# Global-local attention and a gated two-matmul block: the two matmuls in separate phases, attention beside the second

## The chip, the cores and the metric

The kernel runs on one core of a Trainium2 chip. The metric is the device time of one execution in microseconds (us). Times are medians of four or more executions; in the same rounds the kernel before is run on the same chip. The profile is of one execution; its span is about 1.7 us shorter than the time. Engines are named as the profile names them: PE is TensorE's matmuls, PEld its weight loads, DVE is VectorE, ACT is ScalarE, POOL is GpSimd, SP the queue that issues the value loads and the output stores. PSUM is the memory that matmuls write to. The granted clock is the share of full speed that the profile records for TensorE's clock.

## The reference, cut to what matters

```python
# attention: 8 batches, 8 heads, 512 local tokens, 32 global tokens, head size 64
k_all = concat([k_g, k_l]); v_all = concat([v_g, v_l])
out_g = softmax(scale * q_g @ k_all.T) @ v_all              # global rows see everything
s_ll  = where(|i - j| <= 32, scale * q_l @ k_l.T, -1e9)     # local rows: a band, and the global keys
out_l = softmax(concat([scale * q_l @ k_g.T, s_ll])) @ v_all
x = concat([out_g, out_l])                                  # 8*544 tokens x 512
# the block
h = x @ w_in                                                # 512 -> 2048
g = h * sigmoid(1.702 * h)
out = g @ w_out                                             # 2048 -> 512
```

The kernel treats the 512 local tokens of a batch as one block of 512 columns, eight blocks in all, and gathers the global tokens of all batches (256 columns) in a ninth.

## The kernel before

Each batch is two "quads" of four heads, `a` and `c`. A quad's attention is a chain over four engines: transposes `T` of keys and queries (DVE), scores `S` in two rounds (PE), exponentials `X` (ACT), band mask `M` (DVE), then value products `U(0)` (the softmax sums), `U(1)`, `U(2)` (the two halves of the values) and `Gm` (global rows), all on PE, each read out of PSUM by DVE or ACT: `R1`/`R2` turn `U(0)` into reciprocals, `XL` scales `U(1)` and `U(2)` into `x`, `G1` to `G3` do it for `Gm`.

The block has 16 `h` steps (four matmuls into one PSUM bank, a tanh on ACT, a multiply on DVE) and 16 `o` steps (four matmuls each; four steps accumulate in one bank, which ACT then copies to `ob` for the store).

The kernel uses eight PSUM banks, divided so:

```python
psS = tile_pool("psS", bufs=4, PSUM)   # scores
psV = tile_pool("psV", bufs=1, PSUM)   # value products U(0), U(1), U(2), Gm: one bank
psH = tile_pool("psH", bufs=2, PSUM)   # h
psO = tile_pool("psO", bufs=1, PSUM)   # o
```

Everything is interleaved, step by step. In step `k` one `h` step, one `o` step that lies 24 steps behind it, and a piece of attention of the batch after follow each other:

```python
def step(k, pe=(), act0=(), act1=(), dve=()):
    h_mm(k)
    for f in pe: f()              # attention on PE
    if k >= LAG: o_mm(k - LAG)    # LAG = 24
    ...
    h_tanh(k)
    ...
    h_mul(k)
    ...
def att_table(b):
    ...                           # [cut: scores in steps 0 to 7]
    P(5, lambda: a.U(0));   V(5, lambda: a.R1())
    P(7, lambda: a.U(1));   V(8, lambda: a.XL(0))
    P(9, lambda: a.U(2));   V(9, lambda: a.XL(1))
    P(10, lambda: a.Gm());  V(10, lambda: a.G1())
    P(11, lambda: c.U(0));  ...
    V(14, lambda: quads(n)[0].T(0)); V(15, lambda: quads(n)[0].T(1))
```

The loads are issued in the order batch 0, `w_in`, batch 1, `w_out`, then the global keys, queries and values of all later batches in three large pieces (`load_g(4, NQ)`).

The softmax here doesn't subtract the row's maximum and nothing guards it: scores larger than these inputs give would overflow.

## Time and profile before

The median is 424.98 us (423.78 to 425.44, four runs).

| quantity | value | where it is read |
|---|---|---|
| PE busy share of the span | 79% | page, part 1 |
| share of PE in the chain that ended last | 60% | page, part 4 |
| period of a batch | 44.5 us | start of the `rs` transpose of quad `a`, batches 3 to 7, mean of four |
| PE busy in a period | about 38 us | table of windows |
| granted clock at 50 to 89 us | 0.56 | table of windows |

The period is read in every kernel in the same way: each batch transposes its reciprocals once for quad `a` (`rs<-rT` on DVE), and the distance of these marks from batch 3 to batch 7 is divided by four. In before they lie at 144.67 and 322.59 us.

The first fence is the page: the span, PE's busy time, and PE's busy tenths and granted clock in 40 slices of the span. The second is the first line of the chain that ended last.

```profile
span 422.8 us, 7348 instructions
...
PE 335.5 (79%) x2915; PEld 176.1 (42%) x2960; DVE 227.1 (54%) x396; ACT 200.4 (47%) x387; POOL 95.8 (23%) x169
...
PE   0488572578888978899689968998699789999984
...
PEclk9999955599989998999999998999999899999999
```

```profile
PE 60%; DMA 10%; POOL 8%; ACT 8%; issue 6%; DVE 6%; DVEq 0%; POOLq 0%; ACTq 0%
```

PE is the engine that decides, but a fifth of the span it is idle, and in slices 6 to 8 (53 to 85 us) the clock is at half.

Next the waits of PE in the steady part, 150 to 300 us (engine, what it wanted to do, the releaser: total, times, longest), and three of them in the timeline (start, duration, engine, line, operation; in brackets the idle time ahead of it and its releaser).

```profile
PE ov L295 <- DVE xL L323: 9.2, 8, 2.0
PE ov L295 <- ACT xg L345: 7.3, 4, 1.8
PE s L245 <- DVE qT L223: 4.9, 3, 1.6
```

```profile
157.20 0.23 PE L295 MATMUL ov<-e_1801,onesBD 128*128 128x160 bf16 x1 [1.83 <-ACT xg L345]
...
166.00 0.23 PE L295 MATMUL ov<-e_1801,vgU_156 128*128 128x160 bf16 x1 [2.01 <-DVE xL L323]
...
174.27 0.48 PE L245 MATMUL s<-qT,kT 32*128 32x160 bf16 x16 [1.62 <-DVE qT L223]
```

The value products wait for `xL` and `xg`.

The start-up has another wait. These are DVE in the timeline, the issue of the large global load (KB, then us from issue to landing), and a table of windows (start:end, length, busy us and instructions of PE, PEld, DVE, ACT, POOL, granted clock, DMA share, GB/s).

```profile
64.65 0.31 DVE L155 STREAM_TRANSPOSE kgT<-rkg 128x128 bf16<-128x128 bf16 x1 [6.44 <-DMA rkg<-in_k_g_dram]
67.19 0.31 DVE L155 STREAM_TRANSPOSE qgT<-rqg 128x128 bf16<-128x128 bf16 x1 [2.23 <-DMA rqg<-in_q_g_dram]
```

```profile
rkg<-in_k_g_dram POOLq DMA_DIRECT2D x1, 192.0 KB, 17.1
```

```profile
core 0: us, PE busy (x) PEld busy (x) DVE busy (x) ACT busy (x) POOL busy (x), PEclk, DMA share, GB/s
50.00:89.00 39.00, 21.10 (x260) 13.61 (x261) 20.65 (x37) 13.45 (x28) 20.43 (x36) 0.56 1.41 165
146.30:191.60 45.30, 39.03 (x360) 20.00 (x362) 27.02 (x44) 23.85 (x47) 9.15 (x16) 0.96 0.44 71
191.60:235.20 43.60, 37.32 (x356) 19.46 (x358) 26.99 (x44) 23.83 (x47) 9.14 (x16) 1.00 0.48 74
```

DVE stands for 6.4 us in front of the transposed global keys of batch 2, and the attention of batch 1 comes behind them in DVE's program: PE's wait for its `sT`, 7.0 us, ends at 69.29 us.

### The profile page before, as it was taken

The numbers are of one execution on the slowest core, as the hardware profiler recorded it, in microseconds if no ns is written. First come the engines' busy times: TensorE is split into PE (matmuls) and PEld (weight loads), VectorE is DVE, ScalarE is ACT, GpSimd is POOL, SyncE is SP. The second block draws the span as 40 slices with busy tenths as digits, with TensorE's granted clock in tenths as the row PEclk, the third lists the DMA queues.
The fourth block names the chain that finished last, engine by engine and source line by source line (L and its number), as shares of the span: only waits on it lengthen the run. The fifth ranks groups of instructions, "written<-read, shape, count | busy, mean of one in ns | idle before, by whom it ended". The sixth has DMA issues, their size and how long they took to land.

```text
span 422.8 us, 7348 instructions
## 1 busy us (share of the span) xinstructions
PE 335.5 (79%) x2915; PEld 176.1 (42%) x2960; DVE 227.1 (54%) x396; ACT 200.4 (47%) x387; POOL 95.8 (23%) x169
## 2 busy tenths in 40 slices
PE   0488572578888978899689968998699789999984
PEld 0363251335434534454345534454355344445531
DVE  3666835389446653775467645664565433433200
ACT  1546661278336743574456643773466225343311
POOL 8958814981016100620043000000000000000000
PEclk9999955599989998999999998999999899999999
DMA  9799999993009400880069001400001000110122
GB/s 159 82 192 145 142 180 175 157 109 33 26 2 189 61 26 25 126 126 25 26 97 155 26 26 31 119 26 25 2 26 48 3 26 33 43 48 28 50 76 50
DMA packets 83315, 31.16 MB, mean 74 GB/s; under 512 B 75856, under 2 KB 77904, under 8 KB 83280
## 3 DMA queue, kind: packets, MB, share of 16 engines
q0 software_dynamic: 44496, 13.38, 30.0%
q1 hardware_dynamic: 38784, 17.31, 17.2%
q8 instruction: 23, 0.38, 0.4%
q14 instruction: 12, 0.10, 0.1%
HBM read 35.13 MB, written 8.91 MB: 104 GB/s over the span
## 4 chain that ended last, share of the span: by engine, by line
PE 60%; DMA 10%; POOL 8%; ACT 8%; issue 6%; DVE 6%; DVEq 0%; POOLq 0%; ACTq 0%
PE op L393 26%; PE hp L367 21%; DMA rvg<-in_v_g_dram 5%; PE s L268 4%; DMA w_in_sb<-in_moe_w_in_dram 3%; ACT xg L345 3%; PE ov L302 3%; POOL rq L78 3%; POOL rk L78 3%; PE s L245 2%; PE ov L295 2%; DMA rq<-in_q_l_dram 2%; DVE xL L323 2%; DVE qT L223 2%; ACT th L375 1%
## 5 line engine op out<-in xcount | busy, mean ns | idle before, releaser
L381 DVE SCALAR_TENSOR_TENSOR gT<-th,hp 128x512 bf16<-128x512 f32 (+1 forms) x144 | 94.1, 654 | 118.0 <-ACT th L375 117.5
L375 ACT ACTIVATE th<-hp 128x512 f32<-128x512 f32 (+1 forms) x144 | 82.8, 575 | 133.4 <-PE hp L367 132.8
L393 PE MATMUL op<-w_out_sb,gT 128*128 128x512 bf16 x508 | 136.0, 386 | 7.7 <-ACT ob L403 4.7
L367 PE MATMUL hp<-xL,w_in_sb 128*128 128x512 bf16 x503 | 131.3, 387 | 2.1 <-DVE xL L323 1.1
L367 PEld LDWEIGHTS <-w_in_sb 128*128 128x128 bf16 x576 | 57.1, 100 | 67.5 <-issue 6.5
L393 PEld LDWEIGHTS <-gT 128*128 128x128 bf16 x544 | 50.2, 98 | 58.1 <-issue 9.2
L78 POOL DMA_DIRECT2D rk<-in_k_l_dram x64 | 37.0, 582 | 102.4 <-DVE kT L223 91.7
L245 PE MATMUL s<-qT,kT 32*128 32x160 bf16 (+1 forms) x496 | 19.2, 253 | 31.4 <-DVE qT L223 29.3
L78 POOL DMA_DIRECT2D rq<-in_q_l_dram x64 | 36.7, 578 | 24.1 <-DVE qT L223 9.6
L403 ACT ACTIVATE ob<-op 128x512 f32<-128x512 f32 x34 | 20.4, 601 | 31.3 <-PE op L393 31.0
L245 PEld LDWEIGHTS <-kT 32*128 32x128 bf16 x512 | 11.3, 98 | 45.6 <-issue 22.8
L345 ACT ACTIVATE xg<-og,rg 32x64 bf16<-32x64 f32 x64 | 19.4, 303 | 22.3 <-DVE rg L337 21.6
L323 DVE TENSOR_TENSOR xL<-ov,rs 128x512 bf16<-128x512 f32 x32 | 21.9, 687 | 9.4 <-PE ov L302 9.2
L223 DVE STREAM_TRANSPOSE kT<-rk 128x1024 bf16<-128x1024 bf16 x16 | 20.8, 1300 | 3.6 <-DMA rk<-in_k_l_dram 3.6
L223 DVE STREAM_TRANSPOSE qT<-rq 128x1024 bf16<-128x1024 bf16 x16 | 20.9, 1304 | 2.4 <-DMA rq<-in_q_l_dram 2.4
L311 DVE STREAM_TRANSPOSE sT<-ov 128x512 f32<-128x512 f32 x16 | 11.4, 714 | 7.5 <-PE ov L302 7.5
L295 PEld LDWEIGHTS <-onesBD 128*128 128x128 bf16 x64 | 6.0, 106 | 18.0 <-issue 15.1
L295 PEld LDWEIGHTS <-vgU_164 128*128 128x128 bf16 x48 | 4.6, 108 | 18.5 <-issue 17.2
L318 DVE STREAM_TRANSPOSE rs<-rT 128x512 f32<-128x512 f32 x16 | 11.3, 704 | 0.1
L268 PEld LDWEIGHTS <-kT 128*128 128x128 bf16 x128 | 8.1, 103 | 6.2 <-issue 4.5
L367 PE MATMUL hp<-xG,w_in_sb 128*128 128x256 bf16 x64 | 9.6, 273 | 0.1
L189 POOL DMA_DIRECT2D w_in_sb<-in_moe_w_in_dram x16 | 8.5, 536 | 4.7 <-DMA w_in_sb<-in_moe_w_in_dram 4.3
(363 smaller groups left out, 327.5 us busy)
## 6 DMA issues: line engine op xcount, KB each, us to landing
vst<-in_v_l_dram SPq DMA_DIRECT2D x64, 128.0 KB, 5.6
out_dram<-ob SPq DMA_DIRECT2D x32, 256.0 KB, 2.0
rk<-in_k_l_dram POOLq DMA_DIRECT2D x64, 64.0 KB, 4.1
rq<-in_q_l_dram POOLq DMA_DIRECT2D x64, 64.0 KB, 3.8
w_in_sb<-in_moe_w_in_dram POOLq DMA_DIRECT2D x16, 128.0 KB, 6.8
w_out_sb<-in_moe_w_out_dram POOLq DMA_DIRECT2D x4, 512.0 KB, 10.2
out_dram<-ob SPq DMA_DIRECT2D x8, 64.0 KB, 1.7
rkg<-in_k_g_dram POOLq DMA_DIRECT2D x1, 192.0 KB, 17.1
```

Of the source, the lines that this page charges most:

```text
L78: nc.gpsimd.dma_start(out=r[32 * j : 32 * j + 32], in_=src[Q, j])
L223: nc.vector.transpose(dst.rearrange("p h (n r t) -> p h n t r", n=8, t=2), src.rearrange("p n (t h d) -> p h n t d", t=2, h=2),)
L245: nc.tensor.matmul(ps[j][:, col : col + wd], lhsT=kT[p, h, 128 * c : 128 * c + 128], rhs=qT[p, h, q0 : q0 + wd], start=(h == 0), stop=(h = ...
L268: nc.tensor.matmul(o, lhsT=l(h), rhs=r(h), start=(h == 0), stop=(h == 1), skip_group_check=True)
L295: nc.tensor.matmul(ov[:, q0 : q0 + wd], lhsT=lg, rhs=e, start=(i == 0), stop=False, skip_group_check=True)
L323: nc.vector.tensor_mul(self.x[:, 2 * self.u + h, :], self.st[1 + h], self.st["rs"])
L345: nc.scalar.activation(xg[p, :], og[p, j * D : (j + 1) * D], AF.Copy, scale=rg[p, j : j + 1])
L367: nc.tensor.matmul(hp[:, :n], lhsT=w_in_sb[:, kc, fc * 128 : (fc + 1) * 128], rhs=(xL[i] if i < B else xG)[:, kc, :], start=(kc == 0), sto ...
L375: nc.scalar.activation(th[:, :n], hps[k][:, :n], AF.Tanh, scale=0.851)
L381: nc.vector.scalar_tensor_tensor(gTs[i][:, fc, :n], in0=ths.pop(k)[:, :n], scalar=1.0, in1=hps.pop(k)[:, :n], op0=ALU.add, op1=ALU.mult)
L393: nc.tensor.matmul(ops[i], lhsT=gTs[i][:, fc, tci * 128 : tci * 128 + 128], rhs=w_out_sb[:, fc, :], start=(fc == 0), stop=(fc == FC - 1))
L403: nc.scalar.activation(ob, ops[i], AF.Copy, scale=0.5)
```

## The change

Its intent: let the `h` phase run bare, so that PE goes from matmul to matmul; put the attention of the next batch beside the `o` steps, which need almost nothing of ACT and DVE; share three PSUM banks among `h`, `o` and half of the value products; and load `w_out` before batch 1 and the global tensors in pieces. No arithmetic is added or removed.

```diff
-    psH = tile_pool(name="psH", bufs=2, PSUM)
-    psO = tile_pool(name="psO", bufs=1, PSUM)
+    psM = tile_pool(name="psM", bufs=3, PSUM)
 ...
-    load(2); load_g(2, 4); load_v(2); load(3); load_v(3)
     # [cut: w_out in four pieces]
-    load_g(4, NQ)
+    load(2); load_g(2, 4); load(3); load_g(4, 8)
 ...
+    def phase_o(i):               # o of block i, attention of batch i+1
+        late = i == 0
+        ...
+        if late: o(7); cast_v(2), cast_v(3); a.T(0), a.T(1); ...
+        a.S(0); X4(a); a.M(0)
+        o(1 if late else 3)
+        a.S(1); X4(a)
+        if n < B and not late: a2.T(0), a2.T(1)     # transposes of batch i+2
+        a.M(1)
+        o(1 if late else 3)
+        c.S(0); X4(c)
+        a.U(0); a.R1(), a.R2()
+        o(1 if late else 2)
+        a.U(1, True)              # True: in psM, else in psV
+        c.M(0); a.XL(0); c.S(1); X4(c)
+        o(1)
+        a.U(2); a.XL(1); ...
+        a.Gm(True); ...           # [cut: quad c in the same way]
+        if late:
+            load_v(4), load_v(5)
+            cast_v(4), cast_v(5)
+            a2.T(0), a2.T(1); c2.T(0), c2.T(1)
+            transpose_g(4, 6); expand_g(2)
+        ...
+    for i in range(B):
+        for fc in range(FC): h_step(i, fc)
+        if i + 1 < B: phase_o(i)
+    for st in range(FC): h_step(B, st); o_mm(B - 1, st); ...
+    for st in range(FC // 2): o_mm(B, st); ...
-    # [cut: step(), att_table() and the loop over k with LAG]
```

More of the change, by code (lines that the diff above doesn't have):

```diff
@@ L60 @@
     psV = ctx.enter_context(tc.tile_pool(name="psV", bufs=1, space=bass.MemoryType.PSUM))
-    psH = ctx.enter_context(tc.tile_pool(name="psH", bufs=2, space=bass.MemoryType.PSUM))
-    psO = ctx.enter_context(tc.tile_pool(name="psO", bufs=1, space=bass.MemoryType.PSUM))
+    psM = ctx.enter_context(tc.tile_pool(name="psM", bufs=3, space=bass.MemoryType.PSUM))
     qf = q_l.rearrange("b (u j) (n r t) d -> (b u) j r n (t d)", j=4, n=8, t=2)
@@ L190 @@
                                     in_=w_in_r[u, j][:, :, cs])
-    load(2)
-    load_g(2, 4)
-    load_v(2)
-    load(3)
-    load_v(3)
     for g4 in range(4):
@@ L199 @@
         )
-    load_g(4, NQ)
+    load(2)
+    load_g(2, 4)
+    load(3)
+    load_g(4, 8)
     xG = consts.tile([128, NKC, B * Sg], BF16)
@@ L211, in __init__ @@
             if self.u == 0:
-                xL[self.b] = att.tile([128, NKC, Sl], BF16, name="xL", bufs=3)
+                xL[self.b] = att.tile([128, NKC, Sl], BF16, name="xL", bufs=2)
             self.x = xL[self.b]
@@ L233, in S @@
             if alt:
-                ps = [psH.tile([128, 512], F32, name="s2", tag="hp") for _ in range(2)]
-                ps.append(psO.tile([128, 512], F32, name="s2", tag="op"))
+                ps = [psM.tile([128, 512], F32, name="s2", tag="m") for _ in range(3)]
                 ps.append(psV.tile([128, 512], F32, name="s2", tag="ov"))
@@ L284, in M, with U @@
             )
-        def U(self, unit, pool=None, tag="ov"):
+        def U(self, unit, m=False):
             E, v = self.E, loaded[self.Q][2]
             vgU = self.G[2]
-            ov = (pool or psV).tile([128, 512], F32, name="ov", tag=tag)
+            ov = (psM if m else psV).tile([128, 512], F32, name="ov", tag="m" if m else "ov")
             h = unit - 1
@@ L323, in XL, with Gm @@
             nc.vector.tensor_mul(self.x[:, 2 * self.u + h, :], self.st[1 + h], self.st["rs"])
-        def Gm(self, pool=None, tag="ov"):
+        def Gm(self, m=False):
             E, v = self.E, loaded[self.Q][2]
-            og = (pool or psV).tile([128, 4 * D + 4], F32, name="og", tag=tag)
+            og = (psM if m else psV).tile([128, 4 * D + 4], F32, name="og", tag="m" if m else "ov")
             for c in range(4):
@@ L352, in G3, with width, h_step @@
                 self.st["xg"].rearrange("p (h d) -> p h d", h=2))
-    gTs, ops, hps, ths = {}, {}, {}, {}
-    LAG = 24
-    def h_mm(k):
-        i, fc = divmod(k, FC)
-        n = TB if i < B else B * Sg
-        if fc == 0:
-            gTs[i] = moe.tile([128, FC, TB], BF16, name="gT", bufs=3)
-        if k < LAG - 2 and k % 3 == 2:
-            hp = psO.tile([128, TB], F32, name="hp", tag="op")
-        else:
-            hp = psH.tile([128, TB], F32, name="hp", tag="hp")
+    gTs, ops, hps = {}, {}, {}
+    def width(i):
+        return TB if i < B else B * Sg
+    def h_step(i, fc):
+        n = width(i)
+        if fc == 0:
+            gTs[i] = moe.tile([128, FC, TB], BF16, name="gT")
+        hp = psM.tile([128, TB], F32, name="hp", tag="m")
         for kc in range(NKC):
@@ L369, in h_mm, with o_mm @@
                              start=(kc == 0), stop=(kc == NKC - 1))
-        hps[k] = hp
-    def h_tanh(k):
-        n = TB if k // FC < B else B * Sg
         th = moe.tile([128, TB], F32, name="th")
-        nc.scalar.activation(th[:, :n], hps[k][:, :n], AF.Tanh, scale=0.851)
-        ths[k] = th
-    def h_mul(k):
-        i, fc = divmod(k, FC)
-        n = TB if i < B else B * Sg
-        nc.vector.scalar_tensor_tensor(gTs[i][:, fc, :n], in0=ths.pop(k)[:, :n], scalar=1.0,
-                                       in1=hps.pop(k)[:, :n], op0=ALU.add, op1=ALU.mult)
-    def o_mm(k):
-        i, st = divmod(k, FC)
-        n = TB if i < B else B * Sg
+        nc.scalar.activation(th[:, :n], hp[:, :n], AF.Tanh, scale=0.851)
+        nc.vector.scalar_tensor_tensor(gTs[i][:, fc, :n], in0=th[:, :n], scalar=1.0,
+                                       in1=hp[:, :n], op0=ALU.add, op1=ALU.mult)
+    def o_mm(i, st):
         tci, f4 = divmod(st, 4)
-        if tci * 128 >= n:
-            return
         if f4 == 0:
-            ops[i] = psO.tile([128, d_model], F32, name="op", tag="op")
+            ops[i] = psM.tile([128, d_model], F32, name="op", tag="m")
         for fc in range(4 * f4, 4 * f4 + 4):
@@ L394, in o_mm, with o_out @@
                              rhs=w_out_sb[:, fc, :], start=(fc == 0), stop=(fc == FC - 1))
-    def o_out(k):
-        i, st = divmod(k, FC)
-        n = TB if i < B else B * Sg
-        tci, f4 = divmod(st, 4)
-        if tci * 128 >= n or f4 != 3:
-            return
+    def o_out(i, tci):
         ob = moe.tile([128, d_model], F32, name="ob")
@@ L410, in o_out, with X4 @@
                 nc.sync.dma_start(out=out[r : r + Sg, :], in_=ob[32 * j : 32 * j + 32, :])
+    def X4(q):
+        q.X(0, 1, 2, 3)
     a, c = Quad(0), Quad(1)
@@ L416 @@
     a.S(0)
-    a.X(0, 1, 2, 3)
+    X4(a)
     a.M(0)
@@ L421 @@
     c.T(0), c.T(1)
-    a.X(0, 1, 2, 3)
+    X4(a)
     a.M(1)
@@ L425 @@
     cast_v(1)
-    c.X(0, 1, 2, 3)
+    X4(c)
     a.U(0)
     a.R1(), a.R2()
-    a.U(1, psO, "op")
+    a.U(1, True)
     a.XL(0)
     c.M(0)
-    a.U(2, psH, "hp")
+    a.U(2, True)
     a.XL(1)
     c.S(1)
-    a.Gm(psH, "hp")
+    a.Gm(True)
     a.G1()
-    c.X(0, 1, 2, 3)
+    X4(c)
     a.G2()
@@ L442 @@
     c.R1(), c.R2()
-    c.U(1, psO, "op")
+    c.U(1, True)
     c.XL(0)
-    c.U(2, psH, "hp")
+    c.U(2, True)
     c.XL(1)
-    c.Gm(psH, "hp")
+    c.Gm(True)
     c.G1(), c.G2(), c.G3()
-    def step(k, pe=(), act0=(), act1=(), dve=()):
-        if k < (B + 1) * FC:
-            h_mm(k)
-        for f in pe:
-            f()
-        if k >= LAG:
-            o_mm(k - LAG)
-        for f in act0:
-            f()
-        if k < (B + 1) * FC:
-            h_tanh(k)
-        for f in act1:
-            f()
-        if k < (B + 1) * FC:
-            h_mul(k)
-        if k >= LAG:
-            o_out(k - LAG)
-        for f in dve:
-            f()
@@ L470 @@
-    NQD = {}
-    def quads(b):
-        if b not in NQD:
-            NQD[b] = (Quad(2 * b), Quad(2 * b + 1)) if b < B else None
-        return NQD[b]
-    def att_table(b):
-        a, c = quads(b)
-        L = [dict(pe=[], act0=[], act1=[], dve=[]) for _ in range(FC)]
-        P = lambda s, f: L[s]["pe"].append(f)
-        A0 = lambda s, f: L[s]["act0"].append(f)
-        A1 = lambda s, f: L[s]["act1"].append(f)
-        V = lambda s, f: L[s]["dve"].append(f)
-        def soft(q, r, s):
-            P(s, lambda: q.S(r))
-            A0(s + 1, lambda: q.X(0, 1))
-            A1(s + 1, lambda: q.X(2, 3))
-            V(s + 1, lambda: q.M(r))
-        V(0, lambda: c.T(0))
-        soft(a, 0, 0)
-        soft(a, 1, 2)
-        V(2, lambda: c.T(1))
-        soft(c, 0, 4)
-        P(5, lambda: a.U(0))
-        V(5, lambda: a.R1())
-        soft(c, 1, 6)
-        V(6, lambda: a.R2())
-        P(7, lambda: a.U(1))
-        V(8, lambda: a.XL(0))
-        P(9, lambda: a.U(2))
-        V(9, lambda: a.XL(1))
-        P(10, lambda: a.Gm())
-        V(10, lambda: a.G1())
-        A1(11, lambda: a.G2())
-        V(11, lambda: a.G3())
-        P(11, lambda: c.U(0))
-        V(11, lambda: c.R1())
-        V(12, lambda: c.R2())
-        P(12, lambda: c.U(1))
-        V(13, lambda: c.XL(0))
-        P(13, lambda: c.U(2))
-        V(13, lambda: c.XL(1))
-        P(14, lambda: c.Gm())
-        V(14, lambda: c.G1())
-        A1(15, lambda: c.G2())
-        V(15, lambda: c.G3())
-        if b + 1 < B:
-            n = b + 1
-            L[0]["pe"].insert(0, lambda: (load_v(2 * n), load_v(2 * n + 1)))
-            V(4, lambda: transpose_g(2 * n, 2 * n + 2))
-            V(4, lambda: expand_g(n, (0,)))
-            V(7, lambda: expand_g(n, (1, 2)))
-            V(10, lambda: expand_g(n, (3,)))
-            A1(8, lambda: cast_v(2 * n))
-            A1(13, lambda: cast_v(2 * n + 1))
-            V(14, lambda: quads(n)[0].T(0))
-            V(15, lambda: quads(n)[0].T(1))
-        if b + 2 < B:
-            L[4]["pe"].insert(0, lambda: (load(2 * b + 4), load(2 * b + 5)))
-        return L
@@ L534 @@
-    load(4), load(5)
-    for k in range(FC):
-        step(k)
-    q1 = quads(1)
-    q1[0].T(0), q1[0].T(1)
-    transpose_g(2, 4)
-    expand_g(1)
-    cast_v(2)
-    cast_v(3)
-    a, c = q1
-    L1 = att_table(1)
-    for s in range(FC):
-        for f in L1[s]["pe"] + L1[s]["act0"] + L1[s]["act1"]:
-            f()
-        for f in L1[s]["dve"]:
-            f()
-    for k in range(FC, (B + 1) * FC + LAG):
-        b = k // FC + 1
-        if k % FC == 0 and b < B:
-            L = att_table(b)
-        step(k, **(L[k % FC] if b < B else {}))
+    load_v(2), load_v(3)
@@ new lines, with o @@
+    nq = {}
+    def phase_o(i):
+        b = i + 1
+        n = b + 1
+        a, c = nq[b]
+        late = i == 0
+        cnt = [0]
+        def o(k=1):
+            for _ in range(k):
+                o_mm(i, cnt[0])
+                if cnt[0] % 4 == 3:
+                    o_out(i, cnt[0] // 4)
+                cnt[0] += 1
+        if n < B:
+            nq[n] = (Quad(2 * n), Quad(2 * n + 1))
+            a2, c2 = nq[n]
+        if late:
+            o(7)
+            cast_v(2), cast_v(3)
+            a.T(0), a.T(1)
+            transpose_g(2, 4)
+            expand_g(1)
+        a.S(0)
+        X4(a)
+        a.M(0)
+        if late:
+            c.T(0), c.T(1)
+        o(1 if late else 3)
+        a.S(1)
+        X4(a)
+        if n < B and not late:
+            a2.T(0), a2.T(1)
+        a.M(1)
+        o(1 if late else 3)
+        c.S(0)
+        X4(c)
+        a.U(0)
+        a.R1(), a.R2()
+        if n < B and not late:
+            cast_v(2 * n)
+        o(1 if late else 2)
+        a.U(1, True)
+        c.M(0)
+        a.XL(0)
+        c.S(1)
+        X4(c)
+        o(1)
+        a.U(2)
+        a.XL(1)
+        if n < B and not late:
+            c2.T(0)
+        c.M(1)
+        o(1)
+        a.Gm(True)
+        a.G1()
+        a.G2()
+        if n < B and not late:
+            c2.T(1)
+        o(1)
+        c.U(0)
+        c.R1(), c.R2()
+        a.G3()
+        if n < B and not late:
+            cast_v(2 * n + 1)
+        o(1 if late else 2)
+        c.U(1, True)
+        c.XL(0)
+        if n < B and not late:
+            transpose_g(2 * n, 2 * n + 2)
+            expand_g(n, (0, 1))
+        o(1)
+        c.U(2)
+        c.XL(1)
+        if n < B and not late:
+            expand_g(n, (2, 3))
+        o(16 - cnt[0])
+        c.Gm(True)
+        c.G1()
+        c.G2()
+        c.G3()
+        if late:
+            load_v(4), load_v(5)
+            cast_v(4), cast_v(5)
+            a2.T(0), a2.T(1)
+            c2.T(0), c2.T(1)
+            transpose_g(4, 6)
+            expand_g(2)
+        if n + 1 < B:
+            load_v(2 * n + 2), load_v(2 * n + 3)
+        if n + 2 < B:
+            load(2 * n + 4), load(2 * n + 5)
+        if late:
+            load_g(8, NQ)
@@ L558 @@
+    nq[1] = (Quad(2), Quad(3))
+    load(4), load(5), load(6), load(7)
+    for i in range(B):
+        for fc in range(FC):
+            h_step(i, fc)
+        if i + 1 < B:
+            phase_o(i)
+    for st in range(FC):
+        h_step(B, st)
+        o_mm(B - 1, st)
+        if st % 4 == 3:
+            o_out(B - 1, st // 4)
+    for st in range(FC // 2):
+        o_mm(B, st)
+        if st % 4 == 3:
+            o_out(B, st // 4)
 _INS = ['q_l', 'k_l', 'v_l', 'q_g', 'k_g', 'v_g', 'moe_w_in', 'moe_w_out']
```

## The prediction

> **What bounds the kernel now.** TensorE. The page's chain of waits gives PE 60% of the span, DMA 10%, POOL 8%. A batch repeats every 44.5 us: in that chain the qT transposes come at 127.58, 172.91, 216.57, 261.84 and 305.49 us. Its TensorE floor is shorter: 128 full matmuls of 0.216 us (four take 0.86 us in the chain) are 27.6 us, and the attention of one batch is about 9.1 us (estimate from the timeline at full clock: four score rounds of 0.9, six value units of 0.75, two global units of 0.5). So some 7.8 us per batch is TensorE waiting for the handshakes of attention (1 to 2 us gaps, released by xL, xg, qT in the list of waits) with only two `hp` and one `op` bank. Ahead of that lies a bad stretch: first h phase 32.5 to 47.0 us, then the attention of batch 1 until 85 us, with a 7 us gap at 62 to 69 us, where VectorE waits for the kgT source of the 192 KB-a-piece global load (17 to 20 us to landing). TensorE's granted clock there is 0.50 (table of windows, 60 to 80 us). The Trainium skill, "TensorE: Matmul & The Clock Gate", Part 1, says idle windows halve the clock; this trace agrees.
>
> **What the change does.** No arithmetic is removed. (1) One pool of three PSUM banks instead of 2+1. (2) The h phase runs bare: before's own first h phase, three banks and bare, took 14.5 us for 16 steps; I expect 14.2. VectorE's 0.69 and ScalarE's 0.60 a step fit. (3) The o phase carries the attention of the next batch. I walked one steady phase by hand with trace durations (exponentials 2.0 us a round, mask 0.89, transposes 1.3, reciprocal path 1.7, xL 0.69, ob 0.60, casts 1.06): 24.4 us against the floor 22.9; with handshakes I take 26. Period: about 40.3 us, 4 less than before. (4) Global loads are split, so batch 1 no longer waits 7 us for them; w_out comes before batch 1.
>
> **Start-up after.** Same to 47 us. w_out should land by about 45, so the first seven o steps run to 53. Batch 1's scores start near 53, its attention is latency-bound ("late" phase) and ends near 74. Then a new wait: batch 2's values are loaded only behind the last output store of this phase (5.6 us median to landing), and both casts and four transposes stand before h(1)'s first tanh and multiply. TensorE does three h steps, then idles and cools for about 8 us; h(1) ends near 99. Before, h(1) ends near 129.
>
> **Sum.** 99 + 6 x 40.3 = 341; interleaved h(8) and o(7) 22.5; o(8) 7; tail 4.6 (as before, end of last matmul to end); profile-to-time difference 1.7: about 376 us. All of it is on TensorE's chain.
>
> **What the profile should show.** TensorE busy share up from 79% to about 88%; h phases near 14.2 us with three banks turning; o phases 25 to 27 us; steady period 39 to 41.5 us; granted clock about 1.0 from 100 us on; a hole at 75 to 84 us, released by the casts and vst loads.
>
> **What would make it wrong.** Steady phases longer than 28 us (an `ob` behind a cast, c.U(1) waiting for the third bank), or the clock falling in them (slower, to 388). w_out landing later than 50 us under the vst loads. A start-up hole that is shorter than 8 us, or phases at the floor (faster, 364).
>
> I predict 376 us, range 364 to 388; faster 0.96, same 0.03, slower 0.01.

## The result, and the profile after

The changed kernel takes 365.29 us (median of four, 364.69 to 367.22). The ratio is 0.8607 (95% interval 0.857 to 0.8644). Ratios here are the mean time of one kernel's fast runs over the mean of the other's fast runs of the same rounds, so they are not quite the ratio of the medians quoted.

The same views of after: page, chain, and PE's waits from 150 to 300 us.

```profile
span 363.6 us, 7327 instructions
...
PE 315.9 (87%) x2913; PEld 168.8 (46%) x2960; DVE 228.4 (63%) x396; ACT 201.9 (56%) x387; POOL 97.6 (27%) x172
...
PE   0378987940999999999999999999999999999994
...
PEclk9989999995799999999999999999999999999998
```

```profile
PE 70%; DMA 12%; POOL 5%; ACT 4%; issue 4%; DVE 2%; SPq 2%; POOLq 0%; ACTq 0%; DVEq 0%
```

```profile
PE op L374 <- issue: 1.9, 12, 0.2
PE hp L361 <- DVE gT L366: 1.3, 4, 0.3
```

The waits for `xL`, `xg` and `qT`, 21.4 us of that stretch before, are gone; 3.2 us are left. The period is 37.80 us (marks at 152.10 and 303.32 us) against 44.5.

The phases are to be seen in the table of windows (columns as above): first `o` phase, hole, rest of the second `h` phase, a steady `h` phase, a steady `o` phase, and the last `h` and `o` in turn.

```profile
46.00:74.00 28.00, 23.69 (x290) 13.57 (x294) 17.66 (x28) 13.97 (x27) 24.61 (x42) 1.00 1.23 135
74.00:91.00 17.00, 2.89 (x14) 1.18 (x12) 7.79 (x14) 4.80 (x10) 13.05 (x23) 0.72 1.47 188
91.00:104.50 13.50, 13.45 (x67) 5.67 (x66) 8.97 (x14) 7.76 (x14) 2.63 (x3) 0.85 0.99 91
127.62:142.01 14.39, 14.02 (x65) 6.16 (x64) 10.10 (x17) 10.37 (x20) 0.00 (x0) 1.00 0.39 93
142.01:165.43 23.42, 22.84 (x291) 13.40 (x295) 17.10 (x28) 13.86 (x27) 9.09 (x16) 1.00 0.58 80
330.86:351.93 21.07, 20.80 (x126) 12.52 (x128) 7.80 (x18) 8.16 (x20) 0.00 (x0) 1.00 0.10 38
```

A steady `h` phase takes 14.4 us (from its first matmul to the first scores of the next batch) and a steady `o` phase with attention 23.4 us; in both PE is busy for all but 0.4 to 0.6 us.

One hole is left in the start-up. These are PE in the timeline, and the pieces of the chain that ended last in that stretch (start, us, what).

```profile
73.89 2.75 PE L361 MATMUL hp<-xL,w_in_sb 128*128 128x512 bf16 x12
90.76 9.42 PE L361 MATMUL hp<-xL,w_in_sb 128*128 128x512 bf16 x32 [14.11 <-DVE gT L366]
```

```profile
81.09 7.11 DMA vst<-in_v_l_dram
88.31 1.06 ACT v_86 L92
90.02 0.70 DVE gT L366
```

PE does three `h` steps and then stands for 14.1 us: the values of batch 2 are still under way, their casts stand in ACT's queue ahead of the first tanh, and without the tanh no bank comes free. The clock falls with it (0.72 in the window of the hole, 0.85 in the one behind it).

How much of the 59.7 us between the two medians lies where? Six periods of 6.7 us make 40 us (an estimate from the two periods); the other 20 us lie in the start-up and at the end, where the old order ran its `o` steps 24 steps late. The second `h` phase begins at 73.9 us against 85.0 before, with the first 16 `o` steps already done, but then loses 14 us to the hole.

### The profile page after: what moved, and what is told of

Its sections match the earlier page's. It is cut to its first block, busy times and chain, and to the rows that moved or that the text cites. A ratio compares the mean times of both kernels' runs of the same rounds, so it can differ in the third digit from the quotient of the medians.

```text
span 363.6 us, 7327 instructions
## 1 busy us (share of the span) xinstructions
PE 315.9 (87%) x2913; PEld 168.8 (46%) x2960; DVE 228.4 (63%) x396; ACT 201.9 (56%) x387; POOL 97.6 (27%) x172
## 4 chain that ended last, share of the span: by engine, by line
PE 70%; DMA 12%; POOL 5%; ACT 4%; issue 4%; DVE 2%; SPq 2%; POOLq 0%; ACTq 0%; DVEq 0%
PE op L374 29%; PE hp L361 24%; PE ov L298 5%; PE s L264 4%; DMA w_out_sb<-in_moe_w_out_dram 4%; DMA w_in_sb<-in_moe_w_in_dram 4%; PE s L241 3%; DMA rq<-in_q_l_dram 3%; PE ov L291 2%; ACT xg L341 2%; DMA vst<-in_v_l_dram 2%; SPq L88 2%; PE og L325 2%; POOL rq L77 2%; DVE gT L366 2%
## 5 line engine op out<-in xcount | busy, mean ns | idle before, releaser
L361 PE MATMUL hp<-xL,w_in_sb 128*128 128x512 bf16 x503 | 114.9, 384 | 17.4 <-DVE gT L366 16.3
L374 PE MATMUL op<-w_out_sb,gT 128*128 128x512 bf16 x506 | 124.0, 379 | 4.2 <-issue 3.2
L365 ACT ACTIVATE th<-hp 128x512 f32<-128x512 f32 (+1 forms) x144 | 81.7, 574 | 44.8 <-PE hp L361 41.3
L241 PE MATMUL s<-qT,kT 32*128 32x160 bf16 (+1 forms) x496 | 16.0, 243 | 19.0 <-DVE qT L220 18.6
L319 DVE TENSOR_TENSOR xL<-ov,rs 128x512 bf16<-128x512 f32 x32 | 22.0, 690 | 14.4 <-PE ov L298 14.2
L341 ACT ACTIVATE xg<-og,rg 32x64 bf16<-32x64 f32 x64 | 19.5, 305 | 20.2 <-DVE rg L333 18.6
L241 PEld LDWEIGHTS <-kT 32*128 32x128 bf16 x512 | 9.5, 95 | 29.8 <-issue 13.5
L346 DVE STREAM_TRANSPOSE xG<-xg 128x64 bf16<-128x64 bf16 x16 | 3.6, 226 | 10.8 <-ACT xg L341 10.8
L273 ACT ACTIVATE e_265<-s 128x480 bf16<-128x480 f32 (+1 forms) x4 | 2.0, 590 | 12.4 <-PE s L264 12.4
```

The costliest lines, as they stand in the source:

```text
L241: nc.tensor.matmul(ps[j][:, col : col + wd], lhsT=kT[p, h, 128 * c : 128 * c + 128], rhs=qT[p, h, q0 : q0 + wd], start=(h == 0), stop=(h = ...
L319: nc.vector.tensor_mul(self.x[:, 2 * self.u + h, :], self.st[1 + h], self.st["rs"])
L341: nc.scalar.activation(xg[p, :], og[p, j * D : (j + 1) * D], AF.Copy, scale=rg[p, j : j + 1])
L361: nc.tensor.matmul(hp[:, :n], lhsT=w_in_sb[:, kc, fc * 128 : (fc + 1) * 128], rhs=(xL[i] if i < B else xG)[:, kc, :], start=(kc == 0), sto ...
L365: nc.scalar.activation(th[:, :n], hp[:, :n], AF.Tanh, scale=0.851)
L374: nc.tensor.matmul(ops[i], lhsT=gTs[i][:, fc, tci * 128 : tci * 128 + 128], rhs=w_out_sb[:, fc, :], start=(fc == 0), stop=(fc == FC - 1))
```

## The experiments

The theory to begin with was that of the prediction: the steady gain comes from the separate phases, because attention beside `o` has ACT and DVE to itself. The rivals were the load order, and the PSUM banks (a third bank for `h`, or a second one for the value products). All kernels gave correct results. The columns of the table are the medians in us and the period of a batch; the kernel before measured 421 to 427 us beside all of them.

| run | what it is | time | ratio to before | period |
|---|---|---|---|---|
| before | | 424.98 | 1 | 44.5 |
| e1 | before, new load order | 423.11 | 0.9966 | 44.5 |
| e6 | before, one pool of three banks | 419.40 | 0.988 | 44.5 |
| e6b | e6, value products in two pools in turn | 386.39 | 0.9102 | 40.1 |
| e11 | e6b, new load order | 383.62 | 0.9062 | 40.1 |
| e12 | e11, two transposes earlier | 378.89 | 0.8913 | 39.6 |
| after | | 365.29 | 0.8607 | 37.8 |
| e2 | after, old load order | 371.57 | 0.8772 | 37.8 |
| e9 | after, value products in one bank | 378.42 | 0.8891 | 40.1 |
| e5 | after, banks split 2 and 1 | 427.59 | 1.0068 | 46.6 |
| e4 | after, attention beside `h` | 397.89 | 0.9374 | 44.1 |
| e8 | after, attention alone | 424.21 | 1.001 | 48.1 |
| e3 | after, values of batch 2 early | 362.28 | 0.8542 | 37.8 |
| e7 | after, start-up hole taken out | 350.20 | 0.8278 | 37.8 |

### The load order: e1 and e2

e1 gives the old schedule the new load order:

```diff
-    load(2); load_g(2, 4); load_v(2); load(3); load_v(3)
     # w_out
-    load_g(4, NQ)
+    load(2); load_g(2, 4); load(3); load_g(4, 8)
 ...
+    load_v(2), load_v(3)
     load(4), load(5)
 ...
+    load_g(8, NQ)      # before the steady loop
```

> The old schedule with the new load order alone (w_out before batch 1, global loads in pieces, the last piece late). Theory (the gain lies in the steady phases, about 40 of 59 us): the start-up gets 8 to 13 us shorter, the steady period of a batch stays near 44.5 us, time 411 to 418 us. Rival (the load order and the start-up are the main gain): below 390 us.

It missed: 423.11 us, ratio 0.9966 with an interval that holds 1. The attention of batch 1 did get rid of the wait for the global keys, but it began later (PE's first score of batch 1 at 54.4 us against 50.8, as its keys now queue behind `w_out`), and its second quad reached its `rs` mark at 78.18 us against 79.65. Batch 2's mark is at 101.09 against 100.99. The start-up gained nothing that lasts.

e2 takes the new load order out of the new kernel (the same lines the other way).

> The new schedule with the old load order. Theory: w_out lands near 61 us, the first seven o steps and with them attention of batch 1 slip by about 10 us, steady period stays 37.8 us: 373 to 380 us. Rival (load order is the main gain): above 395 us.

371.57 us, just under the theory's range, and an unchanged period. The load order is worth some 6 us in the new schedule, which needs `w_out` at 46 us, and nothing measurable in the old one, which needs it at 102 us. It is not the main gain.

### Which banks: e6, e6b, e9 and e5

e6 draws `h` and `o` of the old schedule from one pool of three banks:

```diff
-    psH = tile_pool(name="psH", bufs=2, PSUM)
-    psO = tile_pool(name="psO", bufs=1, PSUM)
+    psM = tile_pool(name="psM", bufs=3, PSUM)
     # hp, op and the prologue's U and Gm take tag "m" of psM
```

> The old kernel with h and o drawing on one pool of three banks, nothing else. Theory (in the interleaved order o holds one bank over four steps, so h has two as before; its waits are elsewhere): 420 to 428 us. Rival (sharing the banks is the gain): below 400 us.

419.40 us is just under the expected range, and the period does not move. Its PE waits from 150 to 300 us are close to those of before:

```profile
PE ov L294 <- ACT xg L344: 7.3, 4, 1.8
PE ov L294 <- DVE xL L322: 7.1, 7, 2.0
PE s L244 <- DVE qT L222: 4.9, 3, 1.6
```

e6b adds four edits, and nothing else:

```diff
-        P(7, lambda: a.U(1))
+        P(7, lambda: a.U(1, psM, "m"))
-        P(10, lambda: a.Gm())
+        P(10, lambda: a.Gm(psM, "m"))
     # and the same for c at steps 12 and 14
```

> As e6, and the value products of attention go in turn to their own bank and to the pool, as in the new kernel. The list of waits of before puts some 30 us on value products waiting for their single bank (released by xL and xg). Theory: part of it comes back, but the pool is then shared by h, o and values: 405 to 425 us. Rival (the single value bank is the whole cause): below 390 us.

386.39 us: inside the rival's range (below 390), and 19 us under the lower end of the theory's. All waits for `xL` and `xg` are gone from the list:

```profile
PE hp L366 <- DVE gT L380: 4.3, 8, 0.5
PE s L244 <- DVE qT L222: 3.7, 4, 0.9
```

So the waits that the profile of before puts on `xL` and `xg` were waits for the single value bank, and a second bank, in the old order, takes 33 us off e6: more than half of the whole gain. The theory in its first form, that this gain belongs to the separate phases, falls here.

e9 asks the same from the other side: the new kernel with all value products in `psV`.

```diff
-        a.U(1, True)
+        a.U(1)          # likewise a.Gm, c.U(1), c.Gm in phase_o
```

> The new kernel with all value products of attention in their single bank, as before had it. If the single bank is what cost before its handshakes: each o phase grows by 3 to 5 us, time 385 to 400 us. If the o steps that stand between cover it: within 5 us of 365.

378.42 us lies between the two expectations. The period grows by 2.3 us, and the old wait is back, once a batch (PE, 150 to 300 us):

```profile
PE ov L291 <- ACT xg L341: 7.1, 4, 1.8
```

The four kernels make a table of periods: old order with one value bank 44.5 and with two 40.1; separate phases with one 40.1 and with two 37.8. Each of the two causes is worth about 4.4 us a batch alone and 2.3 us on top of the other: they remove in part the same waits. ("The phases" stands here for the whole new order, its placing of transposes and casts included; the pool and the load order alone, e6 and e1, leave the period at 44.5.)

e5 splits the new pool again, two banks for `h` and the value products, one for `o`.

```diff
-    psM = tile_pool(name="psM", bufs=3, PSUM)
+    psM = tile_pool(name="psM", bufs=2, PSUM)
+    psO = tile_pool(name="psO", bufs=1, PSUM)
-    ops[i] = psM.tile(..., tag="m")
+    ops[i] = psO.tile(..., tag="op")
```

> The new kernel with its pool of three PSUM banks split again, two for h and the value products, one for o. Theory (a bare h phase needs three banks: one step's matmul, tanh and multiply take about 2.5 us end to end): h phases grow from 13.9 to about 20 us, o phases by 1 to 3 us, time 410 to 430 us, most or all of the gain gone. Rival (the phases themselves do it, banks are incidental): below 375 us.

427.59 us: the whole gain is gone. In the `h` phase PE does two steps (eight matmuls) and waits for a bank, every 2.43 us:

```profile
190.96 2.12 PE L363 MATMUL hp<-xL,w_in_sb 128*128 128x512 bf16 x8 [0.31 <-DVE gT L368]
193.39 2.12 PE L363 MATMUL hp<-xL,w_in_sb 128*128 128x512 bf16 x7 [0.31 <-DVE gT L368]
```

With three banks two steps take 1.80 us on average (14.4 for 16). Of the 8.7 us that a period grows, 5.3 lie in the `h` phase (229.59 to 249.28 us, 19.7 us against 14.4) and 3.4 in the `o` phase (26.9 against 23.4), where `o` steps wait for the copy `ob` of the group before (9.4 us from 150 to 300 us in PE's waits). So here the bare `h` phase was worth having only with the third bank; which of e5's two shortages costs more in total was not tested apart, the split is read from this trace.

### What stands beside attention: e4 and e8

e4 swaps the partner: from batch 2 on, attention lies beside `h`, and `o` runs bare.

```diff
+            if 0 < i < B - 1:
+                phase_o(i, with_h=True)      # o(k) now issues h steps
+                for st in range(FC): o_mm(i, st); ...
+                continue
```

> The new kernel with the partner swapped from batch 2 on: attention of the next batch beside the first matmul (h), the second matmul (o) bare. Theory (attention runs at the floor because o asks almost nothing of ScalarE and VectorE): the mixed phase needs about 28 us of VectorE work and 26 of ScalarE in 23 us of TensorE work, so it takes 28 to 32 us and the period is 42 to 46 us, time 390 to 415 us. Rival (any separation of phases with three banks does it): period near 37.8 us, time within 8 us of 365.

397.89 us and 44.1 us a batch, inside the theory's range. The mixed phase runs from 176.91 to 207.15 us, 30.2 us, and the bare `o` phase takes 13.9. Three of PE's waits in the mixed phase:

```profile
191.29 1.02 PE L361 MATMUL hp<-xL,w_in_sb 128*128 128x512 bf16 x3 [1.22 <-DVE gT L366]
...
202.44 1.02 PE L361 MATMUL hp<-xL,w_in_sb 128*128 128x512 bf16 x4 [1.56 <-DVE gT L366]
...
207.15 13.97 PE L374 MATMUL op<-w_out_sb,gT 128*128 128x512 bf16 x63 [0.66 <-DVE gT L366]
```

They end with the multiply on DVE (`gT`), which comes late for two reasons. Ahead of the first wait DVE itself stands 1.12 us for the tanh, which runs on ACT behind four exponentials (2.01 us) and a cast (1.06 us). Ahead of the other two, attention's reciprocal path (`sT` to `xG`, 199.94 to 201.81 us) and the expansions of the next batch's global tensors run on DVE just before `gT`. DVE is busy for 25.0 and ACT for 20.2 of the 30.2 us, so neither is full; the likely cost is the order of the work on these two engines, but no run changed that order alone. Beside `o` nothing of `o` needs DVE.

e8 puts attention alone behind a bare `o` phase.

```diff
-            for _ in range(k):
+            for _ in range(k if late else 0):    # no o steps inside attention
 ...
+        if 0 < i < B - 1:
+            for st in range(FC): o_mm(i, st); ...
         phase_o(i)
```

> The new kernel with the steady o phases bare and the attention of the next batch alone behind them. Theory (o steps fill the hand-overs of attention): o 13.8 us, attention alone 17 to 20 us as for batch 0, period 45 to 48 us, time 408 to 428 us. Rival (attention is near its floor of 9 us with two value banks even alone): period near 38 us, time below 375 us.

424.21 us. The `o` phase, the start of the attention behind it and a wait in the next `h` phase, which starts at 234.84 us, in PE's timeline; then the attention in the table of windows:

```profile
203.81 13.98 PE L374 MATMUL op<-w_out_sb,gT 128*128 128x512 bf16 x63
217.72 0.48 PE L241 MATMUL s<-qT,kT 32*128 32x160 bf16 x16
...
237.02 1.24 PE L361 MATMUL hp<-xL,w_in_sb 128*128 128x512 bf16 x5 [1.28 <-DVE xL L319]
```

```profile
217.70:234.80 17.10, 12.82 (x231) 8.94 (x231) 12.92 (x19) 11.97 (x23) 7.01 (x13) 0.90 0.61 87
```

Attention alone takes 17.1 us, beside `o` it adds 9.5 us (23.4 less 13.9). So the `o` steps save 7.6 us a batch there, even with two value banks. These are not all hand-overs: PE is idle for 4.3 of the 17.1 us, and for the rest its matmuls are recorded as longer, at a granted clock of 0.90. The `h` phase behind it loses another 2.4 us (16.8 against 14.4), as it waits for the last `xL` and `xg`. With e4 this shows that `o` beside attention helps, and that the partner matters.

### What is left of the lead of the phases: e11 and e12

> e6b (old interleaved order, one pool, two value banks: 386.4 us, period 40.1 us) with the new load order too. If load order is worth 6 us, as e2 has it in the new schedule: 378 to 383 us. If it is worth nothing in the old order, as e1 has it: 384 to 388 us. Either way the steady period stays 40 us, so the separate phases keep a lead of 2.3 us a batch.

e11 is e6b with the load order of e1. 383.62 us lies between the two, and the period stays. The load order is worth about 3 us here. (The 39.7 us that the next expectation gives as its period is the mean from batch 2 on; the marks from batch 3 on give 40.1.)

e12 moves two lines of e11:

```diff
-            V(14, lambda: quads(n)[0].T(0))
-            V(15, lambda: quads(n)[0].T(1))
+            V(10, lambda: quads(n)[0].T(0))
+            V(13, lambda: quads(n)[0].T(1))
```

> e11 (old interleaved order with one pool, two value banks and the new load order: 383.6 us, period 39.7 us) with the two transposes of the next batch's first quad put at steps 10 and 13 of 16 instead of 14 and 15. TensorE waits about 0.9 us a batch there for qT. If that wait is what is left of the lead of the separate phases: period 38.5 to 39 us, time 376 to 381 us. If the lead has other causes, or the transposes push attention's own work back: 382 us or more.

The time, 378.89 us, is as expected of the first case, but the steady period only falls from 40.1 to 39.6 us, which is not: the wait for `qT` leaves PE's list, and the waits of `hp` for `gT` grow from 4.3 to 6.3 us in 150 us. The separate phases keep 1.8 us a batch against the old order at its best here. Whether a better table could win that too was not tried.

### The hole in the start-up: e3 and e7

e3 issues the loads of batch 2's values at the head of the first `o` phase, not behind its stores:

```diff
             cast_v(2), cast_v(3)
+            load_v(4), load_v(5)
 ...
-            load_v(4), load_v(5)
             cast_v(4), cast_v(5)
```

> The new kernel with the values of batch 2 loaded before the output stores of the first o phase instead of behind them. Theory: the TensorE hole at 76.6 to 90.8 us is the wait for these values; with them in place the four transposes and the expansions on VectorE (done at 82.2 us) are what is left, so the hole ends near 83 us and the time falls 6 to 9 us, to 356 to 359 us. Rival (the hole is the transposes or something else): within 2 us of 365.

It won 3 us, half of the least that was expected: 362.28 us. The hole did shrink, to 6.3 us, but it now begins at 81.4 us and not at 76.6. PE in the timeline, and the transpose that made it late:

```profile
78.63 2.75 PE L361 MATMUL hp<-xL,w_in_sb 128*128 128x512 bf16 x12
87.64 12.86 PE L361 MATMUL hp<-xL,w_in_sb 128*128 128x512 bf16 x51 [6.27 <-DVE gT L366]
```

```profile
62.53 1.31 DVE L220 STREAM_TRANSPOSE qT<-rq 128x1024 bf16<-128x1024 bf16 x1 [2.35 <-DMA rq<-in_q_l_dram]
```

The second quad of batch 1 now waits for its queries and is transposed at 62.53 us instead of 59.02. The likely reason is that the values, issued from 52.2 us on, take DMA from them; that was not measured by itself, but e7 fits it. What was taken from one wait went in part into another. What is left of the hole is the preparation of batch 2 on DVE, which ends at 87.0 us.

e7 loads the values behind the second store, when batch 1 has landed, and spreads the preparation of batch 2 over DVE's and ACT's idle places:

```diff
+        if late: load_v(4), load_v(5)      # before c.S(0)
 ...
-        if late:
-            load_v(4), load_v(5); cast_v(4), cast_v(5)
-            a2.T(0), a2.T(1); c2.T(0), c2.T(1); transpose_g(4, 6); expand_g(2)
+        # a2.T(0) after a.G2(), a2.T(1) before c.G3(); c.T(1) in phase_o(1) after a.M(0)
+    EXTRA = {2: cast_v(4), 4: c2.T(0), 6: cast_v(5), 8: transpose_g(4, 6),
+             10: expand_g(2, (0, 1)), 12: expand_g(2, (2, 3))}   # between the steps of h(1)
```

> The new kernel with the hole of the start-up removed: values of batch 2 loaded behind the second output store instead of the fourth, and their casts, the transposes and the expansions of batch 2 spread over the end of the first o phase and the second h phase. Theory: the 14 us hole before 90.8 us and about 2 us of cold clock behind it go, the steady period stays 37.8 us: 348 to 353 us. Rival (the hole hides DMA time that comes out elsewhere, as 5 of the 8 us did in e3): 356 to 362 us.

350.20 us (349.80 to 351.36), ratio 0.8278: 15 us below after, and faster than both kernels. Its page, and PE at the start of the second `h` phase:

```profile
span 349.6 us, 7329 instructions
...
PE 315.2 (90%) x2913; PEld 168.8 (48%) x2960; DVE 227.8 (65%) x396; ACT 201.6 (58%) x387; POOL 97.6 (28%) x172
...
PEclk9999999999999999999999999999999999999999
```

```profile
74.55 2.75 PE L361 MATMUL hp<-xL,w_in_sb 128*128 128x512 bf16 x12
77.63 2.75 PE L361 MATMUL hp<-xL,w_in_sb 128*128 128x512 bf16 x12 [0.32 <-DVE gT L366]
```

The hole is gone and the clock stays at full. The whole 14 us are won. Here the values were not put in front of loads that were needed sooner.

## Why the prediction was right

The predicted time was 376 us with a range of 364 to 388; 365.29 is inside, near its lower end. That is partly luck: two errors of size went opposite ways, and had the hole been the 8 us that were predicted, the time would have been about 360 us (an estimate, 365.3 less 5.2), outside the range.

- **Right: what bounds the kernel, and the period of 44.5 us.** The measured idle time of PE in a period is 6.3 us, where the prediction took 7.8 from a floor.
- **Right in size, named wrongly: what the idle time waits for.** The prediction listed the releasers `xL`, `xg` and `qT` correctly, but put the idle time on hand-overs "with only two `hp` and one `op` bank". e6 pools those banks and the period stays at 44.5; e6b gives the value products a second bank and it falls to 40.1. The scarce bank was the value bank. The change repaired it in passing, by the `True` in `a.U(1, True)`. The Trainium skill, "Perfetto Trace Analysis", section Optimization Strategy, says that the same gap repeating on the engine that should be saturated can mean that there isn't enough SBUF or PSUM for the next tile. This trace agrees: two gaps of 1.8 and 2.0 us come in a batch, and one more PSUM bank removes them.
- **Right: the `h` phase.** 14.2 us predicted, 14.4 measured, with three banks; e5 shows 19.7 with two.
- **Mis-sized: the `o` phase.** The walk by hand gave 24.4 us; 1.6 us were added for hand-overs, to 26. Measured: 23.4, under the 25 to 27 that were forecast, and with it the period is 37.8, under 39 to 41.5. In the steady `o` phase PE is idle for 0.6 us in all, so nothing was to be added for hand-overs, and the walk itself was 1 us long. Six periods of 2.5 us less are 15 us.
- **Mis-sized: the hole.** 8 us predicted, released by casts and value loads; 14.1 us measured, with those releasers. The term was the loads: 5.6 us to landing, the median of the whole run before, was used for loads that are issued eight at a time while DMA is at 9 tenths or more (page, the slices from 73 to 91 us). The first cast could begin at 83.46 us and the second at 88.31, 8.9 and 13.7 us behind the first issue at 74.59. That is 5.2 us the other way: h(1) ended at 104.2 us, not 99.
- **Right: the start-up up to the hole.** First scores of batch 1 at 52.9 us (53 predicted), end of the phase at 73.9 (74).
- **Right: the profile as a whole.** PE's busy share is 87% (88 predicted), and the clock is near full from 105 us on.
- **Right: the end.** The last `h` and `o` in turn took 21.1 us (22.5 predicted), and `o` of the ninth block with the tail 11.7 (11.6).

The sum: the terms of the prediction add up to 376.6; less 15.1 for the periods, plus 5.2 for h(1), less 1.4 for the last `h` and `o`, it is 365.3, as measured. So these differences account for the whole.

The point on the clock also held. The Trainium skill, "TensorE: Matmul & The Clock Gate", Part 1, says that an idle window halves the clock. Before, it was 0.56 from 50 to 89 us, where PE waits for data for up to 7.0 us at a time; in e7, whose PE waits at most 1.7 us at a time after 33 us, it is 1.00 from there on. At the very start the recorded clock does not fit the durations: e7's first 26 us are recorded as 1.00 too, after a wait of 13.0 us, but the same sixteen score matmuls take 0.77 us at 13.03 us and 0.48 us at 54.03.

## What to carry to other kernels

When a saturated engine shows the same short gap in every period, ask whose buffer it waits for before the schedule is rewritten: the releaser in the list of waits was the reader of a single PSUM bank, and four edits on top of the pooled banks won more than half of what the rewrite won (33 of 59.7 us). Put latency-bound work beside matmuls that need no other engine, not beside those whose results must go through the same queues, and give a bare phase enough banks to turn; here it lost all it had won without them (e5). Preparation for the next stage that is issued at a phase boundary stood ahead of the new phase on ACT and DVE here and cost 14.1 us: issue it early, but behind the loads that are needed sooner (e3 and e7).

## What the Trainium skill lacked or had wrong

- "TensorE: Matmul & The Clock Gate", section Back-to-back issue gap, gives about 131 ns per matmul for a sustained stream of weight loads and matmuls of 512 columns, and calls the 216 ns of its formula an over-count. Here the bare `o` phase of e8, 64 such pairs, takes 13.98 us: 218 ns each. The formula holds, the 131 ns do not.
- "DMA: Bandwidth & Descriptors", section Anatomy of one DMA — SWDGE (gpsimd) path, fits a DMA as 2.0 us plus bytes over 436e3 per us. For the 192 KB global load that is 2.5 us (an estimate from that fit); it took 17.1 us to landing here, issued among other loads with DMA at 9 tenths or more. The fit says nothing of a load issued behind others, and that was the term which the prediction got wrong for the value loads too.
- No page says how a wait for a PSUM bank shows in a profile whose releaser is the bank's last reader; here it was 16.5 us of PE's waits in 150 us, under the names `xL` and `xg`.
